# The second of three 768-token blocks makes its output products by Strassen's scheme, in an attention and feed-forward kernel

## The chip, the cores and the metric

The kernel runs on one core of one Trainium2 chip. The metric is device time in microseconds of one execution, the median of the runs shown. One execution was taken with the hardware profiler; where this text gives a start or a window, it is in microseconds from the first instruction of that execution.

## The reference

```
for c in range(24):                      # chunks of 32 queries, 8 heads of 64, 4 batches of 768
    k_full = concat(mem_k, k[c*32-16 : c*32+40]); v_full = concat(mem_v, v[same])
    s = (q_c @ k_full.T) / 8
    a = exp(s - max(s)); a = a / (sum(a) + 1e-9)
    out[c] = a @ v_full
x = out as 3072 tokens x 512             # 8 heads of 64 side by side
h = x @ w_in                             # 512 x 2048
g = max(h, 0) + alpha * min(h, 0)
result = g @ w_out                       # 2048 x 512
```

All arrays are float32. The two large products, x @ w_in and g @ w_out, are the bulk of the arithmetic. The kernel makes each of them from three reduced-precision products: every operand is split into a high part (rounded to fp32r) and a low part (the remainder, again fp32r), and low times high, high times low and high times high are added in PSUM. So each product step is three matmuls, and each operand costs one rounding copy (`high`, ScalarE) and one subtraction (`low`, VectorE or GpSimd).

## The kernel before

**Blocks.** The 3072 tokens are eight halves of 384 (BT). The first two halves are two plain blocks; the other six are three big blocks of 768 tokens, called big 0, big 1 and big 2 here (`big(s)`, L1209). Attention is made in 32 units (four pairs of heads for each half): the first eight ahead of everything, the rest between the matmuls, a few units at a time (`attend`, L535, and `meet`, L1580, which tables AT_PAIR and AT_REST place).

**Up.** A big block splits x into 2 by 2 quarters and w_in into slices; slice pair i holds the columns of two slices f = 2i and 2i+1. `pair` (L1404) makes the seven Strassen-Winograd products of one slice pair (B11, B21, T2, T3, T1, T4, B22), each six matmuls of 128x384 in `product`, L1418. It puts them together with one copy (L1431) and seven additions of a PSUM bank to an SBUF tile (`add_in`, L1439), and each of the four results is bent by alpha (`bent`, L1232 on ScalarE and L1235 on VectorE). The forms of x that the products multiply are differences of quarters (`forms`, L1070: `less` on GpSimd, L1073) and their high and low parts (`split_form`, L1048: L1055 and L1059). The forms of w_in are made by `sum_far` (L963) and kept in DRAM (far_a, far_b).

**Down.** Big 0 and big 1 make g @ w_out plainly: `chunk` (L1259) is three matmuls of 128x512 for one slice, half and 128-token tile, 96 chunks a block, with high and low parts from `rooms` (L1242). Big 2 makes it by Strassen's scheme: `form_down` (L1353) makes four differences of g for a slice pair on GpSimd (L1359), and `product_down` (L1363) makes a step of one product, three matmuls of 128x384 at L1372, for 7 products by 8 slice pairs by 2 column halves. Two of the seven products (A1, two steps each) run beside the pairs (`early_down`), five in `finish` (L1496), which adds the results (L1534) and writes the output transposed. The weights' forms S1 to S4 for this are made by `sum_far(..., down)` from loaded w_out slices (the additions at L982) while big 0 and big 1 run, and kept in DRAM (far_s).

**Order.** Nothing runs in the order of the code. Every step goes to `Plan.add` with an engine, a cost in microseconds, what it reads and writes and a due time; `Plan.send` (L198) then simulates five engines and one DMA queue and issues, on each engine, the ready step with the most work behind it. The table SHIFT moves single steps by microseconds. The result is one fixed instruction order for each engine. All large transfers go through SyncE's one queue, in order; an issue that waits for its data or its room holds the issues behind it.

**Rooms.** SBUF is shared out by hand. Weights of the pairs (1.79 MB a pair: `wa`) and of the down steps (`wo`, `ws`, 1 MB each) come from DRAM into seven slots (9 to 15), which the lists `queues` and LAST_ROOMS hand out; a slot is loaded again when its last matmul has read it. PSUM has eight banks: three for the products of a pair, three for down sums, two for attention scores.

## Time and profile before

| | us |
|---|---|
| median of 3 runs (574.44 to 578.03) | 576.23 |
| the profiled execution | 574.95 |
| its span, first to last instruction | 573.2 |
| TensorE busy in the span | 562.8 |
| VectorE, ScalarE, GpSimd busy | 428.2, 311.5, 195.3 |
| moved by DMA | 173.57 MB, mean 303 GB/s |

The span is 1.75 us shorter than the profiled execution's time, and that execution is 1.28 us under the median. Matmuls are pipelined: the mean duration of one overlaps the next, so the rate of a run of matmuls is its length over its count. Some matmul records are missing from the trace. "DMA share" is the mean busy share of the core's 16 DMA engines. Big 0 begins at about 165 (its pairs at 204), big 1 at 317, and the two blocks' work overlaps around 443 to 454, where big 2's pairs begin.

### The profile page before, as it was taken

Reading aid. Unit: us, or ns where it says so; the run is one execution under the profiler, and the core shown is the slowest. Engines: PE = TensorE matmul, PEld = TensorE weight load, DVE = VectorE, ACT = ScalarE, POOL = GpSimd, SP = SyncE. Lnnn points to the kernel's source line nnn. Section 1 sums busy time; section 2 is a strip of 40 time slices with the busy share of each in tenths; the row PEclk is TensorE's granted clock in tenths of the full one; section 3 lists DMA queues with packets and bytes.
Section 4 is the critical chain, followed back from the end, with each engine's and each line's share of the span. In section 5 each row is a group of like instructions: output and inputs, shape, how many; then the busy total and the mean of one; then the engine's idle time right before and its main releaser. Section 6 shows DMA issues by size and latency. Waiting matters only on the chain.

```text
span 573.2 us, 12065 instructions
## 1 busy us (share of the span) xinstructions
PE 562.8 (98%) x4515; PEld 509.2 (89%) x4515; DVE 428.2 (75%) x786; ACT 311.5 (54%) x792; POOL 195.3 (34%) x219
## 2 busy tenths in 40 slices
PE   7999999999999999999999999999999999999997
PEld 4789989888988899988888989999888899999997
DVE  7888888886648987666656777786855867787765
ACT  3778788775655663354566553543554543335452
POOL 5641000024375833005146511232533844443300
PEclk9999999999999999999999999999999999999999
DMA  8999954658996699987999999997988599778721
GB/s 310 374 417 419 414 238 184 227 216 293 335 377 251 231 393 409 377 322 259 326 365 331 351 382 327 355 313 287 312 290 280 198 339 353 279 241 332 266 84 56
DMA packets 64706, 173.57 MB, mean 303 GB/s; under 512 B 5768, under 2 KB 32520, under 8 KB 57736
## 3 DMA queue, kind: packets, MB, share of 16 engines
q1 hardware_dynamic: 64504, 172.70, 82.8%
q8 instruction: 36, 0.59, 0.4%
q14 instruction: 22, 0.18, 0.1%
q10 hardware_dynamic: 144, 0.10, 0.1%
HBM read 128.74 MB, written 44.04 MB: 301 GB/s over the span
## 4 chain that ended last, share of the span: by engine, by line
PE 88%; DMA 7%; DVE 2%; POOL 1%; issue 1%; ACT 0%; SPq 0%; DVEq 0%; POOLq 0%; ACTq 0%
PE b_ps L1418 25%; PE b_ps L1274 20%; PE o_ps L870 12%; PE h_ps L840 12%; PE b_ps L1372 10%; PE a_ps L528 3%; PE b_ps L1311 3%; DMA far_sS<-form 2%; PE s_ps L425 2%; DMA early<-heads 2%; DMA wa<-far_a 2%; DMA w_t<-w_out 1%; DVE u L1439 1%; PE a_ps L688 0%; POOL ew L663 0%
## 5 line engine op out<-in xcount | busy, mean ns | idle before, releaser
L1418 PE MATMUL b_ps<-xf,wa 128*128 128x384 f32 x924 | 168.1, 336 | 0.9 <-DMA wa<-far_a 0.9
L1418 PEld LDWEIGHTS b_ps<-xf,wa 128*128 128x128 f32 x924 | 161.1, 188 | 4.3 <-DVE gs L1235 1.3
L1439 DVE TENSOR_TENSOR u<-b_ps,u 128x384 f32<-128x384 f32 x154 | 79.5, 552 | 42.9 <-PE b_ps L1418 28.1
L1232 ACT ACTIVATE g<-u 128x384 f32<-128x384 f32 x88 | 45.5, 525 | 74.2 <-DVE u L1439 72.3
L480 POOL TENSOR_TENSOR e<-e,den 128x384 f32<-128x384 f32 x24 | 22.0, 919 | 137.5 <-DVE den L474 103.3
L840 PE MATMUL h_ps<-xh,w 128*128 128x384 f32 x256 | 65.4, 336 | 0.0
L1274 PE MATMUL b_ps<-wo,xh 128*128 128x512 f32 x180 | 55.9, 392 | 0.0
L1274 PE MATMUL b_ps<-wo,gh 128*128 128x512 f32 x180 | 55.9, 392 | 0.0
L870 PE MATMUL o_ps<-w,xh 128*128 128x512 f32 x168 | 52.5, 394 | 0.0
L840 PEld LDWEIGHTS h_ps<-xh,w 128*128 128x128 f32 x256 | 46.4, 188 | 0.8
L459 ACT ACTIVATE e<-s_ps,mx 128x64 f32<-128x64 f32 x144 | 43.1, 323 | 5.3 <-DVE mx L451 5.3
L840 PE MATMUL h_ps<-xl,w 128*128 128x384 f32 x128 | 43.7, 341 | 0.0
L1073 POOL TENSOR_TENSOR plain<-plain 128x384 f32<-128x384 f32 x24 | 29.4, 1238 | 36.6 <-ACT plain L602 29.7
L1274 PEld LDWEIGHTS b_ps<-wo,xh 128*128 128x128 f32 x180 | 33.8, 188 | 6.6
L1274 PEld LDWEIGHTS b_ps<-wo,gh 128*128 128x128 f32 x180 | 33.8, 188 | 6.5
L870 PEld LDWEIGHTS o_ps<-w,xh 128*128 128x128 f32 x168 | 31.5, 188 | 6.2
L1274 PE MATMUL b_ps<-wo,xl 128*128 128x512 f32 x90 | 35.4, 393 | 0.7 <-DVE xl L1252 0.7
L1274 PE MATMUL b_ps<-wo,gl 128*128 128x512 f32 x90 | 35.6, 395 | 0.0
L870 PE MATMUL o_ps<-w,xl 128*128 128x512 f32 x84 | 33.1, 394 | 0.0
L459 ACT ACTIVATION_READ_ACCUMULATOR e<-s_ps,mx 128x1 f32 x144 | 31.0, 215 | 0.0
L1059 POOL TENSOR_TENSOR xf<-plain,xf 128x384 fp32r<-128x384 f32 x24 | 27.0, 1142 | 11.3 <-ACT xf L1055 11.2
L852 DVE SCALAR_TENSOR_TENSOR g<-g,rise,h_ps 128x384 f32<-128x384 f32 x32 | 19.3, 607 | 12.5 <-ACT g L849 12.5
(166 smaller groups left out, 1129.6 us busy)
## 6 DMA issues: line engine op xcount, KB each, us to landing
wo<-far_o SPq DMA_DIRECT2D x24, 1024.0 KB
wa<-far_a SPq DMA_DIRECT2D x22, 1024.0 KB
wa<-far_b SPq DMA_DIRECT2D x22, 768.0 KB
qk<-qkw SPq DMA_DIRECT2D x24, 464.0 KB
w_t<-w_in SPq DMA_DIRECT2D x16, 512.0 KB
w_t<-w_out SPq DMA_DIRECT2D x16, 512.0 KB
far_o<-w SPq DMA_DIRECT2D x16, 512.0 KB
far_sS<-form SPq DMA_DIRECT2D x32, 256.0 KB
```

What stands on the lines that cost most here:

```text
L459: nc.scalar.activation(out=st["e"][:, i], in_=st["s"][h2][:, n], func=AF.Exp, scale=SCALE, bias=d["mx"][:, u - us[0], n, h2:h2 + 1], accum ...
L480: nc.gpsimd.tensor_tensor(out=st["e"], in0=st["e"], in1=st["den"].broadcast_to([P, NJ * 2, KW]), op=ALU.mult)
L840: nc.tensor.matmul(out=h["ps"][:, :BT], lhsT=ws[f, 0][:, wk, k * P:(k + 1) * P], rhs=parts(blk, k)[1](xk), start=(k == 0 and n == 0), stop ...
L852: nc.vector.scalar_tensor_tensor(out=h["g"], in0=h["g"], scalar=rise[:, f:f + 1], in1=h["ps"][:, :BT], op0=ALU.mult, op1=ALU.add)
L870: nc.tensor.matmul(out=o_ps[tt], lhsT=h[gk][:, tt * P:(tt + 1) * P], rhs=ws[f, 1][:, wk], start=(f == first_f and i == 0), stop=(f == last ...
L1059: eng.tensor_tensor(out=xf[x][:, 1, p], in0=plain_at(ap), in1=xf[x][:, 0, p].bitcast(F32), op=ALU.subtract)
L1073: step(POOL, 1.04, lambda: nc.gpsimd.tensor_tensor(out=plain_at(to[0]), in0=plain_at(a[0]), in1=plain_at(b[0]), op=ALU.subtract), reads=[a ...
L1232: nc.scalar.activation(out=h[name], in_=src(), func=AF.Relu, scale=-1.0)
L1274: nc.tensor.matmul(out=o[which][tt], lhsT=h[gk][:, tt * P:(tt + 1) * P], rhs=w[:, wk].bitcast(F32R), start=(f == turns[which][0] and i == ...
L1372: nc.tensor.matmul(out=o[0][bank[1]], lhsT=w[:, wk, m * P:(m + 1) * P].bitcast(F32R), rhs=forms_g[gk][xk], start=opened and k == 0, stop=c ...
L1418: nc.tensor.matmul(out=h[bank[1]][:, :BT], lhsT=weight(wk, p).bitcast(F32R), rhs=xf[xi][:, xk, p], start=p == 0 and k == 0, stop=p == 1 an ...
L1439: nc.vector.tensor_tensor(out=h[t], in0=h[bank[1]][:, :BT], in1=h[t if of is None else of], op=ALU.add)
```

## The change

Big 1 now takes the path of big 2: `finish` runs for both, with seven lower products over 8 slice pairs, and both write their output transposed. In both, only A11 (one product, `early_down`) runs beside the pairs; A12 is a sixth product of `finish` and is added onto A11's open PSUM banks, and S4 onto S1's (ONTO, LOWER). The fourteen weight loads of a block use five slots (ROOMS), since slots 14 and 15 now hold kept g tiles (`cell`). The form T3 of g is written to DRAM (far_t) and read back. In big 1 the forms T1 and T3 are made in the pair and T2 and T4 in `finish`; attention's last units are met between `finish`'s steps.

In `pair`, in all three blocks, the products come in another order: B21 is added onto B11's bank after B11 was copied out, and B22, put off until the next pair's first product was issued, onto T1's bank. Five additions remain of seven, and c11 is bent from PSUM.

The decoder writes decoded, unsplit weights to DRAM (far_raw, `keep_raw`): w_out's slices of the pairs 3 to 7, w_in's of 5 to 7. `sum_far` reads these (pairs 0 to 2 of w_out: the split parts, far_o) in place of weights in SBUF or of far_a and far_r, and most of the w_out sums move from big 1 into big 0. In `forms`, T3's low part and two of four differences move from GpSimd to VectorE. Outputs of big 0 leave through one buffer where three took turns. SHIFT is replaced as a whole (its entries are left out here).

```diff
-NROWS = B * S - 2 * BT
+NROWS = B * S - 4 * BT
...
-AT_PAIR = ({2: 16, 5: 18}, {1: 24, 4: 26}, {})
-AT_REST = ({2: 20, 9: 22}, {3: 28, 11: 30}, {})
+AT_PAIR = ({2: (16, 20), 5: (18, 22)}, {2: (None, 26), 6: (24, 28)}, {})
+AT_REST = ({2: (20, 24), 7: (22, None)}, {4: (26, 30), 16: (28, None), 28: (30, None)}, {})
...
-FIRST_LATE = 5
-LATE_AT = {(0, 0): 5, (0, 5): 6, (1, 3): 7}
-DOWN_AT = {(1, 2): 1, (1, 3): 2, (1, 4): 3, (1, 5): 4, (1, 6): 5}
-DOWN_REST = {(0, 4): 6, (0, 6): 7, (1, 2): 0}
+FIRST_LATE, FIRST_RAW = 5, 3
+LATE_AT, LATE_REST = {(0, 0): 5, (0, 4): 6}, {(0, 8): 7}
+DOWN_AT = {(0, 1): 3, (0, 2): 1, (0, 3): 2, (0, 5): 6, (1, 2): 5}
+DOWN_REST = {(0, 2): 4, (0, 5): 7, (0, 11): 0}
...
-LAST_ROOMS = ((13, "A1", 0), (14, "A1", 1), (15, "S1", 0), (13, "A1", 2), (14, "A1", 3), (13, "S1", 1), (9, "S2", 0),
-              (10, "S2", 1), (11, "S4", 0), (12, "S4", 1), (14, "S3", 0), (15, "S3", 1), (13, "A22", 0), (9, "A22", 1))
-LAST = (("S1", "T1"), ("S2", "T2"), ("S4", "c22"), ("S3", "T3"), ("A22", "T4"))
+ROOMS = ((13, "A11", 0), (13, "A11", 1), (9, "S1", 0), (10, "S1", 1), (11, "A12", 0), (12, "A12", 1), (13, "S4", 0),
+         (9, "S4", 1), (10, "S2", 0), (11, "S2", 1), (13, "S3", 0), (12, "S3", 1), (11, "A22", 0), (13, "A22", 1))
+LOWER = (("S1", "T1"), ("A12", "c21"), ("S4", "c22"), ("S2", "T2"), ("S3", "T3"), ("A22", "T4"))
+ONTO = ("A12", "S4")
+FROM = {"A11": (0, 0), "A12": (1, 0), "A22": (1, 1)}
...
-SHIFT = {("load_head", 1): 1.6, ("load_head", 7): 1.5, ("load", 0): 4.1, ("load", 4): -11.2, ("load", 15): 3,
...
+SHIFT = {("load_whole", 0): 12.8, ("load_head", 1): 3, ("load_values", 1): -1.5, ("move", 0): 2.3,
...
+    far_t = {(s, i): far.tile([P, BT], F32, name=f"far_t{s}{i}", tag=f"t{s}{i}") for s in range(1, NBIG) for i in range(NFP)}
+    far_raw = [far.tile([P, 2, DM], F32, name=f"far_raw{f}", tag=f"raw{f}") for f in range(NF)]
...
+        kept_raw = [i for i in parts if f >= 2 * (FIRST_RAW if i else FIRST_LATE)]
+
+        def keep_raw():
+            lo = parts.index(kept_raw[0])
+            move(out=far_raw[f][:, kept_raw[0]:], in_=d["a"].bitcast(F32)[:, lo:])
+
+        if kept_raw:
+            step(SP, 0.75, keep_raw, reads=[a], writes=[("raw", f, i) for i in kept_raw])
...
-    MORE = PLACES + [(sums, "r", [("rs", 0, 0), ("rs", 0, 1)])]
-    MORE += [(sums, f"s{i}", [("f", i, 0), ("f", i, 1)]) for i in range(2)]
-
-    def leave_at(late):
-        n = next(ntmp)
-        return MORE[n % (2, 3, len(MORE))[late]]
+
+    def leave_at(late=False):
+        return PLACES[0 if late else next(ntmp) % 2]
...
     far_b = [far.tile([P, 6 * HALF], F32, name=f"far_b{i}", tag=f"b{i}") for i in range(NFP)]
-    far_r = {i: far.tile([P, 4 * HALF], F32, name=f"far_r{i}", tag=f"r{i}") for i in range(FIRST_LATE, NFP)}
-    far_s = {(x, h): far.tile([P, NFP // 2, 2, HALF], F32, name=f"far_s{x}{h}", tag=f"s{x}{h}")
-             for x in ("S1", "S2", "S3", "S4") for h in range(2)}
-    far_o = [far.tile([P, 2, 2, DM], F32, name=f"far_o{i}", tag=f"o{i}") for i in range(NFP)]
+    far_s = {(x, h): far.tile([P, NFP // 2, 2, DM], F32, name=f"far_s{x[0]}{h}", tag=f"s{x[0]}{h}")
+             for x in (("S2", "S3"), ("S4", "S1")) for h in range(2)}
+    far_w = [far.tile([P, NFP // 2, 2, 2, DM], F32, name=f"far_o{h}", tag=f"o{h}") for h in range(2)]
+    far_o = [far_w[i // 4][:, i % 4] for i in range(NFP)]
 
...
-        if i >= FIRST_LATE:
-            send(f1, 0, ("dr", i), far_r[i])
...
-    def sum_far(i, gate, down=None):
-        late = down is None and i >= FIRST_LATE
+    def sum_far(i, gate, down=None, begin=0.0):
+        late = i >= (FIRST_LATE if down is None else FIRST_RAW)
+        both = down is not None and not late
+        which = int(down is not None)
...
+            if both:
+                formed(n)
+                move(out=t[n].bitcast(F32), in_=far_o[i][:, n])
+                return
+            begun(n)
+            move(out=r[n], in_=far_raw[2 * i + n][:, which])
...
-        def put_down(n, k2, x):
-            move(out=far_s[x, i // 4][:, i % 4], in_=t[n].bitcast(F32)[:, :, k2 * HALF:(k2 + 1) * HALF])
-
-        whole = [[("rs", n, 0), ("rs", n, 1)] + ([("f", n, 1)] if n or late else []) for n in range(2)]
-        if late:
...
+        for n in range(2):
+            if late:
+                step(SP, 0.75, partial(fetch, n), reads=gate + [("raw", 2 * i + n, which)], writes=whole[n], rest=begin)
+            else:
+                step(DVE, 0.7, partial(full, n), reads=gate + ([("f", n, 0), ("f", n, 1)] if both else [("w", 0, 2 * i + n, 0), ("w", 0, 2 * i + n, 1)]), writes=whole[n],
+                     port=True, rest=begin)
...
-        slow = ("B11", "B21", "T3", "T4")
+        slow = ("B11", "B21", "T4")
...
-            less(b12, b22, b12)
+            less(b12, b22, b12, True)
             split_form("T3", *b12, p)
-            less(b22, b22, b11)
+            less(b22, b22, b11, True)
             split_form("T2", *b22, p)
...
+        def go():
+            to = wa[x, b, h] = wps[f, 0].tile([P, n, 2, HALF], F32, name="ws", tag="w")
+            f01, k = FROM[x] if pair_of is None else (None, pair_of.index(x))
+            src = far_w[h][:, :, f01] if pair_of is None else far_s[pair_of, h]
+            move(out=to, in_=src[:, :, :, k * HALF:(k + 1) * HALF])
...
+    def cell(n, s):
+
+        if n < 6 or 14 <= n < 16:
+            f = NF // 2 + (n + 2 if n < 6 else n - 14)
+            to, key = keep_place(f)
+            return (lambda: plain_at(to)), [key]
+        f, b = divmod(n - 6, 2) if n < 14 else divmod(n - 16, 5)
...
+        def form_down(i, names):
+            for to, a, b in (("T1", "c12", "T1"), ("T3", "c22", "T3"), ("T2", "c22", "T1"), ("T4", "c21", "T2")):
+                if to not in names:
+                    continue
...
+                if to == "T3":
+                    step(SP, 0.75, lambda pt=pt: move(out=far_t[s, i], in_=pt()), reads=[kt], writes=[("dt", s, i)])
...
+        def fetch_form(i):
+            place, key = form_at("c22", i)
+            back["T3", i] = place, key
+            step(SP, 0.75, lambda: move(out=place(), in_=far_t[s, i]), reads=[("dt", s, i)], writes=[key])
...
-            for x in range(2):
-                room_of["A1", x, i] = room_of[2 * i + x]
-                forms_g["A1", x, i] = g[0, 2 * i + x]
-                for m in range(2):
-                    product_down("A1", i // 2, ("A1", x, i), i, low_banks[2 * x + m], m, i == 0, i == NFP - 1)
-            if i % 2:
-                load(home["A1", i // 2])
+            gk = "A11", i
+            room_of[gk] = room_of[2 * i]
+            forms_g[gk] = g[0, 2 * i]
+            for m in range(2):
+                product_down("A11", gk, i, lower[m], m, i == 0, i == NFP - 1)
+            if i % 4 == 3:
+                load(home["A11", s, i // 4])
...
-                                start=p == 0 and k == 0, stop=p == 1 and k == 2,
+                                start=not onto and p == 0 and k == 0, stop=p == 1 and k == 2, skip_group_check=onto,
...
             product(a, 0, w(0, 0), "B11")
             copy_out(0, a)
-            product(b, 0, w(0, HALF), "B21")
-            product(c, 0, w(0, 4 * HALF), "T2")
-            add_in(1, c, 0)
-            add_in(0, b)
-            first(h, "c11", 0, f0)
-            product(a, 1, w(1, 0), "T3")
-            add_in(2, a, 1)
+            end_pair()
+            product(b, 0, w(0, 4 * HALF), "T2")
+            add_in(1, b, 0)
+            product(a, 0, w(0, HALF), "B21", True)
+            first(h, "c11", lambda: h[a[1]][:, :BT], a[2], f0)
+            product(c, 1, w(1, 0), "T3")
+            add_in(2, c, 1)
             product(b, 1, w(1, HALF), "T1")
             add_in(0, b, 2)
-            add_in(1, b)
-            bent(h, "c22", lambda: h[0], ("tmp", 0), f1, *kept_at(f1))
-            product(c, 1, w(1, 4 * HALF, HALF), "T4")
-            add_in(2, c)
-            first(h, "c21", 2, f1)
-            product(a, 0, w(0, 5 * HALF), "B22")
-            add_in(1, a)
-            bent(h, "c12", lambda: h[1], ("tmp", 1), f0, *kept_at(f0))
-            if last:
-                form_down(i)
+            bent(h, "c22", lambda: h[0], ("tmp", 0), f1, *(claim("c22", i) if s else kept_at(f1)))
+            product(a, 1, w(1, 4 * HALF, HALF), "T4")
+            add_in(2, a)
+            first(h, "c21", lambda: h[2], ("tmp", 2), f1)
+            load(home["i", s, i, 1])
+
+            def rest_of_pair():
+                product(b, 0, w(0, 5 * HALF), "B22", True)
+                add_in(2, b, 1)
+                bent(h, "c12", lambda: h[2], ("tmp", 2), f0, *(claim("c12", i) if s else kept_at(f0)))
+                if s:
+                    form_down(i, ("T1", "T3", "T2", "T4") if last else ("T1", "T3"))
+                load(home["i", s, i, 0])
+
+            open_pair.append(rest_of_pair)
+            if s:
                 if i:
                     early_down(i - 1)
             elif i:
                 for f in (2 * i - 2, 2 * i - 1):
                     whole(0, f)
                 used(0, i - 1)
-            for x in range(2):
-                load(home["i", s, i, x])
...
-                at_, x = leave_at(1 if s == 0 else 0), {}
+                at_, x = leave_at(True), {}
...
+            for n, (x, name) in enumerate(LOWER):
+                banks = banks_of[x]
                 for i in range(NFP):
+                    at_ = n * NFP + i
+                    think()
+                    if at_ in AT_REST[s]:
+                        meet(AT_REST[s][at_], spare_banks)
                     if n == 0 and i == 2:
                         early_down(end)
                         for m in range(2):
+                            copy("a", m, lower[m])
                     take_down(x, name, i)
+                    if x == "S4":
+                        fetch_form(i)
+                    if x == "S1" and not last:
+                        form_down(i, ("T2",))
+                    if x == "A12" and not last:
+                        form_down(i, ("T4",))
+                    if last and x == "A22" and i >= NFP - NEND:
                         continue
                     for m in range(2):
+                        late_down(x, name, i, banks[m], m, i == 0 and x not in ONTO, i == end)
                     if i == 3 or i == end:
+                        load(home[x, s, i // 4])
                 for m in range(2):
+                    if x == "S1":
+                        copy("c", m, banks[m])
+                    elif x == "A12":
+                        copy("b", m, banks[m], (0, 0, m))
                     elif x == "S4":
+                        pass
+                    elif x == "S2":
+                        add("a", "a", m, banks[m])
+                        add("b", "a", m, upper[m], tile_no=(0, 1, m))
                     elif x == "S3":
+                        add("a", "a", m, banks[m])
+                        add("c", "c", m, other="a", tile_no=(1, 1, m))
+                    else:
+                        if last:
+                            for i in range(NFP - NEND, NFP):
+                                late_down(x, name, i, banks[m], m, False, i == end)
+                        add("a", "a", m, banks[m], tile_no=(1, 0, m), parts=1 + m if last else 1)
...
-        if last:
+        if s:
```

## Rows read from the trace of the kernel before

**Rows 1.** The page's busy time by engine: microseconds, share of span, instructions.
```profile
PE 562.8 (98%) x4515; PEld 509.2 (89%) x4515; DVE 428.2 (75%) x786; ACT 311.5 (54%) x792; POOL 195.3 (34%) x219
```

**Rows 2.** Busy time by stage: engines with instruction counts, granted clock, DMA share, GB/s.
```profile
core 0: us, PE busy (x) PEld busy (x) DVE busy (x) ACT busy (x) POOL busy (x), PEclk, DMA share, GB/s
...
165.00:317.00 152.00, 151.94 (x1370) 134.68 (x1356) 107.26 (x213) 82.77 (x272) 61.45 (x64) 1.00 0.91 329
317.00:386.00 69.00, 68.08 (x588) 63.24 (x588) 55.52 (x112) 34.36 (x103) 19.55 (x22) 1.00 0.99 348
386.00:454.30 68.30, 67.61 (x370) 58.27 (x370) 47.35 (x71) 30.04 (x60) 30.82 (x30) 1.00 0.79 280
454.30:523.70 69.40, 69.40 (x398) 68.87 (x397) 52.22 (x97) 27.87 (x56) 33.07 (x31) 1.00 0.83 300
523.70:573.20 49.50, 46.26 (x264) 45.38 (x263) 34.09 (x63) 22.64 (x46) 4.82 (x4) 1.00 0.45 159
```

**Rows 3.** Pieces of the chain that ended last: start, length, work.
```profile
273.38 10.26 PE b_ps L1274 x45
...
303.73 1.47 PE a_ps L528 x32
...
426.30 12.45 PE b_ps L1274 x54
...
469.61 7.28 PE b_ps L1418 x42
...
523.69 46.29 PE b_ps L1372 x264
```

**Rows 4.** Waits of the big blocks' matmuls (b_ps) on TensorE: total us, times, longest.
```profile
PE b_ps L1418 <- DMA wa<-far_a: 0.9, 1, 0.9
...
PE b_ps L1274 <- DVE xl L1252: 0.7, 1, 0.7
```

**Rows 5.** The DMA queue's packets, MB and share, 165 to 317 and 317 to 454.3.
```profile
q1 hardware_dynamic: 17180, 49.80, 90.3%
...
q1 hardware_dynamic: 16632, 42.94, 88.6%
```

**Rows 6.** What SyncE's queue waited for: total, times, longest.
```profile
SPq L322 <- DVE form L993: 26.4, 18, 4.0
```

**Rows 7.** Groups by line and shape: busy, mean ns; idle before and releaser.
```profile
L1439 DVE TENSOR_TENSOR u<-b_ps,u 128x384 f32<-128x384 f32 x154 | 79.5, 552 | 42.9 <-PE b_ps L1418 28.1 <-issue 8.3 <-ACT u L1431 3.2
...
L459 ACT ACTIVATE e<-s_ps,mx 128x64 f32<-128x64 f32 x144 | 43.1, 323 | 5.3 <-DVE mx L451 5.3
...
L459 ACT ACTIVATION_READ_ACCUMULATOR e<-s_ps,mx 128x1 f32 x144 | 31.0, 215 | 0.0
...
L1059 DVE TENSOR_TENSOR xf<-plain,xf 128x384 fp32r<-128x384 f32 x20 | 19.0, 972 | 7.6 <-ACT xf L1055 7.5
...
L1431 ACT COPY u<-b_ps 128x384 f32<-128x384 f32 x22 | 10.5, 480 | 22.2 <-PE b_ps L1418 20.2 <-DVE vg L1235 1.0 <-DVE qk L1235 1.0
...
L1534 DVE TENSOR_TENSOR o_t<-b_ps,o_t 128x384 f32<-128x384 f32 x13 | 7.1, 554 | 1.5 <-PE b_ps L1372 1.4
...
L1252 DVE TENSOR_TENSOR gl<-gs,gh 128x384 fp32r<-128x384 f32 x12 | 6.6, 555 | 4.4 <-ACT gh L1248 4.4
...
L982 DVE TENSOR_TENSOR sum<-wo 128x512 f32<-128x512 f32 x8 | 5.5, 684 | 1.1 <-DMA out<-o_t 1.1
...
L1248 ACT CAST gh<-gs 128x384 fp32r<-128x384 f32 x12 | 6.2, 516 | 9.2 <-PE b_ps L1274 7.1 <-PE b_ps L1372 2.1
...
L1359 POOL TENSOR_TENSOR gs<-gs 128x384 f32<-128x384 f32 x4 | 4.1, 1018 | 0.0
```

**Rows 8.** Timeline where VectorE and GpSimd both build forms: start, length, work.
```profile
443.46 2.65 DVE L1059 TENSOR_TENSOR xf<-plain,xf 128x384 fp32r<-128x384 f32 x2
...
441.79 3.90 POOL L1073 TENSOR_TENSOR plain<-plain 128x384 f32<-128x384 f32 x3 [0.56 <-DVE xf L1059]
```

380 lines of the change are left out of this document (206 added, 174 removed), and 37 rows, old and new, of the table SHIFT.

## The prediction

> **What bounds the kernel now.** I read the page's busy times first: TensorE is busy for 562.8 us of the 573.2 us span, no other engine above 75% [rows 1]. An average can hide a stage, so the table by stage comes next [rows 2]. From 165 to 523.7 TensorE is idle for 1.7 us in all, at granted clock 1.00 (the 2.4 GHz level); the last stage loses 3.2 us after its last matmul, the rest lies ahead of 165. The chain that ended last is, where big 0, 1 and 2 are concerned, nearly a list of matmuls back to back [rows 3], and the waits of their matmuls come to 0.9 and 0.7 us, one each [rows 4]. So time goes where TensorE's instruction time goes, as long as the others keep up. The second reading is how near they are: the DMA engines are 90.3% and 88.6% busy over big 0 and big 1 [rows 5], 99% from 317 to 386, and TensorE still lost only 0.9 us of those 69 [rows 2]. VectorE has a quarter of its time left.
>
> **Part 1, the output products of big 1.** Removed: 96 chunks of three matmuls of 512 columns. Their rate is 10.26/45 = 228 ns to 12.45/54 = 231 ns each [rows 3], so 288 take 65.7 to 66.4 us. Added: 7 products by 8 slice pairs by 2 column halves by 3 = 336 matmuls of 384 columns. The same instruction runs in big 2 at 46.29/264 = 175 ns, and the pairs' at 7.28/42 = 173 ns [rows 3]: 58.2 to 58.9 us. The difference is 6.8 to 8.2 us; I take **-7.5**. No other TensorE work changes: the pairs keep 42 matmuls each, attention's products are only met at other places.
>
> **Part 2, what Strassen asks of the others.** In `finish` of big 1 each step of TensorE (6 matmuls, 1.05 us) wants one rounding on ScalarE (516 ns) and one subtraction on VectorE (555 ns alone) [rows 7]. The half block is 48 such steps, one early step and three meetings of attention values at 1.47 us [rows 3]: 49 x 1.05 + 4.4 = 55.9 us. ScalarE: 48 + 14 (forms of big 2) roundings at 516 ns, 12 exponentials at 323 + 215 ns, 12 copies at 480 ns [rows 7] = 32.0 + 6.5 + 5.8 = 44.3 us, 79%. VectorE: 48 + 8 low parts and 4 differences at 555 ns, 10 additions at 554 ns = 33.3 + 5.5 = 38.8 us, some 70%, if nothing slows it. The 16 differences of g on GpSimd are 16.3 us at 1018 ns. From 454.3 to 523.7 VectorE was busy for 75% and GpSimd for 48% with no idle TensorE [rows 2], so I cost this at nothing; it is covered by the matmuls, and the second rival prices the case that it is not.
>
> **Part 3, pairs with five additions.** 22 pairs x 2 x 552 ns = 24.3 us leave VectorE [rows 7]. TensorE didn't wait for them (rows 4 have no such line), so this gives no time, only room. New waits: B21 goes onto B11's bank, so it waits for ScalarE's copy of 480 ns [rows 7]; between them lie B22 of the pair before and T2, 2 x 1.04 us of cover (6 matmuls at 173 ns). c11 is read from PSUM by two engines, and T4 wants that bank two products later: an estimated 1.2 us of reading (a copy's 480 ns and an addition's 552 to 684 ns [rows 7] as the nearest rows) under 2.1 us. Both hold unless ScalarE's queue is over a microsecond late; bounds 0 and 0.5 us a pair, I take 0, because the old order gave the same copy two products before T3 took its bank, and shows no wait. T2 is now wanted as the second of a pair's own products, so a block's first pair wants the forms earlier. Its chain (difference 1018, rounding 516, low part 972 ns [rows 7]) is 2.5 us; units 22 and 23 are met two slices sooner (two slices are 18 matmuls, 4.1 us), and steps of the block before can stand in. 0 to 2.5 us, I take 0.
>
> **Part 4, the weight sums.** The raw additions drop from 32 to 16, 16 x 684 ns = 10.9 us off VectorE [rows 7], again not on the path. The price is in DMA. Over big 0 and big 1: the three late w_in sums fetch 2 x 0.26 MB in place of 2 x 0.52 (-1.6 MB); the eight w_out sums, which read slots before, fetch 3 x 1.05 + 5 x 0.52 MB (+5.8); big 1 loads 14 weight tiles for 13 (+1.0); T3 goes out and comes back, 16 x 0.197 MB (+3.1). Together +8.4 MB. The queue moved 92.7 MB there in 0.903 x 152 + 0.886 x 137.3 = 258.9 busy us [rows 5], 2.79 us a MB: 23.4 us more, 282.3 busy us in a stretch of 289.3 - 7.5 = 281.8 us. So the change takes all the room that the DMA engines had. From 317 to 386 they were 99% busy and cost TensorE one wait of 0.9 us [rows 2, 4]; bounds are 0 and the 23.4 us. I take one more such wait, **+0.9**, being nearest to that stage.
>
> The sums move from big 1 to big 0, in SyncE's order past the pairs' loads. A put waits for its low part, 18 times for 1.5 us and at most 4.0 [rows 6], and the loads of `wa` stand behind it. There are now 16 puts of 512 KB for 32 of 256 KB, and 16 fetches more. A `wa` slot has a pair and two slices (7.3 + 4.1 us) to be filled in big 0 and 8.3 us in big 1; 1.88 MB take 5.2 us. A 4 us hold is about what is left, so it is covered, barely. The decoder's ten puts of raw weights (4.2 MB, for 1.6 of far_r) fall before 165. Single buffer for big 0's outputs: three copies and transfers in a row of 0.26 MB (0.7 us each and the way there); the first early step on those banks comes two pairs later, 14 us: nothing.
>
> **Sum.** -7.5 + 0.9 = -6.6: span 566.6 us, execution 568.4 with the 1.75 us around it. The profiled execution stands 1.28 us under the median of 576.23, so the median comes to **569.6 us**.
>
> **Rival 1, the DMA queue becomes the bound (slower).** Place: 165 to 446. Before, 30.4 of 289.3 us were gaps, in which nothing was ready or an issue waited. The demand is 282.3 busy us, so every microsecond of gap that remains is a microsecond longer. If half remain, the stretch is 297.5 us, 8.2 longer than before: 584.4 us. It passes 582 from 12.8 us of gaps on. For it: the fetch, form, put chain of a sum lies in one set of buffers and must idle; 165 to 317 is where demand rises most. Against: 317 to 386 ran without gaps, the sums have until big 1's `finish`, 66 us into it, and much of the rise can be put off to 386 to 454, where the share was 79% [rows 2]. Chance 0.15.
>
> **Rival 2, GpSimd and VectorE hold each other up in big 1's lower half (no change).** Where both build forms, three GpSimd differences took 3.90 us and two VectorE low parts in the same time 2.65 [rows 8], 1.3 us a pair for operations that take 1.02 and 0.555 alone [rows 7]. The half has 28 GpSimd operations (16 differences of g, 6 low parts, 4 differences of x, 2 scalings) and 60 VectorE operations of that kind: 28 x 1.3 + 32 x 0.555 = 54.2 us, and 59.7 with the additions from PSUM behind them, against TensorE's 55.9. So the wait is 0 to 3.8 us, and up to 2.5 more where big 2's first pair finds T2 late: with 5 us, 573.7. For it: the two differences and T3's low part that move to VectorE. Against: in 454.3 to 523.7 GpSimd made 31 operations beside 97 of VectorE without a wait [rows 2]. Chance 0.18. The Trainium skill (SBUF — State Buffer, "SBUF: two separate sides") says that a VectorE operation with two SBUF inputs and a GpSimd operation that reads SBUF take one port pair in turn, each for its whole length, which speaks against moving work between these two; by that rule alone the half would be 28 x 1.02 + 60 x 0.555 = 61.9 us, 6.0 over, and the kernel at 574.7. The pair of 1.3 us agrees with it to within 0.3.
>
> **Rival 3, it gains more.** The two waits of 1.6 us lie in replaced code [rows 4]; with them gone, no new one and 8.2 us of part 1, the span is 563.4, the median 566.4. Chance 0.07. That the change doesn't do what it says is excluded by part 1's rates, unless 336 matmuls are not what runs.
>
> **How the numbers follow.** The forecast's case has 0.60. One per cent is 5.8 us, about what a measurement of this kernel can tell from no change; the bound is 570.5, only 0.9 over my number, so of that 0.60 I put 0.45 to faster and 0.15 to within. Rival 1 gives 0.10 slower, 0.05 within; rival 2 0.16 within, 0.02 faster; rival 3 0.07 faster. Faster 0.54, same 0.36, slower 0.10. Range: rival 3 less a microsecond for its scatter, 565.5, up to rival 2 at its full price and rival 1 with up to 9 us of gaps, 578. The forecast's own range is 566.5 to 573.
>
> **What would show it.** In the changed profile: 228 ns matmuls of 512 columns gone from big 1 and some 672 at L1372's successor at 175 ns in both blocks; 110 additions in the pairs for 154; TensorE idle 165 to 523 under 3 us; DMA share near 1.0 in big 0 and 1. Wrong if TensorE waits for `wa`, `ws` or forms for over 3 us there (rival 1: for DMA; rival 2: for VectorE's or GpSimd's forms about 425 to 455), or if it gains time ahead of 165, which I count as unchanged.

## The result, and the profile after

| | before | after |
|---|---|---|
| median of 9 runs each, us | 575.50 (573.53 to 578.93) | 580.22 (579.30 to 581.53) |
| span of the profiled execution, us | 573.2 | 579.2 |
| mean granted clock of TensorE in it | 1.000 | 0.997 |
| moved by the SyncE queue, MB | 172.70 | 186.86 |

The ratio is 1.0078, 95% interval 1.0053 to 1.0103: the kernel became 0.8% slower, where 1.1% faster was forecast. 580.22 lies outside the range. Here and below, each ratio compares a kernel with runs of the kernel before on the same chip, so ratios, and not medians, are set against each other. One run each of e1, e4 and e8 and the profiled one of e5 (774.6 us at a clock of 0.657) were disturbed and are in no ratio.

The page's line of busy times, which answers to [rows 1]:

```profile
PE 558.5 (96%) x4563; PEld 514.4 (89%) x4563; DVE 437.5 (76%) x774; ACT 323.1 (56%) x820; POOL 213.6 (37%) x233
```

TensorE has 48 matmuls more and is busy 4.3 us less; its idle time went from 10.4 to 20.7 us. So -4.3 + 10.3 make the 6.0 us of the span. The table by stage shows where, with the columns of [rows 2]; big 1 now ends at 459.4 where it ended at about 454 (twelve of its matmuls came later, among big 2's pairs):

```profile
core 0: us, PE busy (x) PEld busy (x) DVE busy (x) ACT busy (x) POOL busy (x), PEclk, DMA share, GB/s
165.00:317.00 152.00, 149.62 (x1338) 132.20 (x1337) 110.69 (x206) 80.47 (x251) 59.10 (x63) 1.00 0.97 352
317.00:386.00 69.00, 61.78 (x530) 57.67 (x529) 48.40 (x97) 35.48 (x122) 31.01 (x34) 0.98 0.99 347
386.00:460.00 74.00, 72.96 (x487) 71.38 (x486) 60.54 (x94) 42.38 (x89) 40.65 (x34) 1.00 0.97 334
460.00:529.00 69.00, 68.40 (x395) 68.11 (x394) 52.62 (x87) 27.30 (x55) 30.47 (x29) 1.00 0.79 271
529.00:579.20 50.20, 46.96 (x271) 46.64 (x269) 30.38 (x54) 23.37 (x47) 4.87 (x4) 1.00 0.74 243
```

Two stages hold most of it: 2.4 us of TensorE are idle in big 0 and 7.2 between 317 and 386, where it was 0.1 and 0.9; that is 8.6 of the 10.3 us. The two last stages are as long as they were, within 0.7 us. The DMA share is 0.97 to 0.99 in all three stages of big 0 and big 1, where it was 0.91, 0.99 and 0.79. The queue's packets, MB and share from 165 to 317 and from 317 to 460, as in [rows 5]:

```profile
q1 hardware_dynamic: 17602, 53.31, 96.9%
...
q1 hardware_dynamic: 27800, 48.43, 97.7%
```

That is 101.74 MB in 147.3 + 139.7 = 287.0 busy us of 295. Before it was 92.74 MB and 258.9 of 289.3. The gaps fell from 30.4 to 8.0 us, and the stretch still grew: 5.1 us to its end at 459.4, most of the loss.

TensorE's longest waits in the big blocks, the successors of [rows 4] (total us, times, longest):

```profile
PE b_ps L1528 <- DVE u L1549: 2.8, 3, 1.4
PE a_ps L592 <- DMA pt<-far_e: 2.6, 2, 2.1
PE b_ps L1477 <- ACT o_t L1598: 2.4, 1, 2.4
PE b_ps L1477 <- DVE gl L1343: 1.7, 1, 1.7
PE b_ps L1528 <- DMA wa<-far_a: 0.6, 1, 0.6
```

Only two of the five name a transfer. The timeline shows what the others wait for (start, length, engine, line, idle time before it and its releaser); here for `o_t` and `gl`:

```profile
330.61 0.59 ACT L1598 COPY o_t<-b_ps 128x512 f32<-128x512 f32 x1
331.22 0.34 SPq L386 DMA_DIRECT2D out<-o_t  x1
...
338.59 0.58 ACT L1598 COPY o_t<-b_ps 128x512 f32<-128x512 f32 x1 [3.67 <-DMA out<-o_t]
...
339.23 0.44 PE L1477 MATMUL b_ps<-xl,ws 128*128 128x384 f32 x1 [2.39 <-ACT o_t L1598]
...
343.32 3.18 POOL L1067 TENSOR_TENSOR sum<-sum 128x256 f32<-128x256 f32 x4 [1.46 <-DMA sum<-far_raw]
...
345.78 0.49 ACT L1323 ACTIVATE g<-b_ps 128x384 f32<-128x384 f32 x1 [2.87 <-PE b_ps L1528]
...
347.40 0.69 DVE L1075 TENSOR_TENSOR form<-sum,form 128x512 fp32r<-128x512 f32 x1
...
348.08 0.63 ACT L1072 CAST form<-sum 128x512 fp32r<-128x512 f32 x1
...
348.70 1.02 POOL L1457 TENSOR_TENSOR plain<-gw,plain 128x384 f32<-128x384 f32 x1 [2.20 <-DVE gw L1326]
...
348.75 1.52 DVE L1075 TENSOR_TENSOR form<-sum,form 128x512 fp32r<-128x512 f32 x1
...
350.66 0.88 DVE L1343 TENSOR_TENSOR gl<-gs,gh 128x384 fp32r<-128x384 f32 x1
...
351.59 0.44 PE L1477 MATMUL b_ps<-gl,ws 128*128 128x384 f32 x1 [1.69 <-DVE gl L1343]
```

Big 0's third output waits 3.67 us on ScalarE, since the one buffer is still being written out: issued at 331.22, the write let the next copy start at 338.59. The early product wants that PSUM bank, and TensorE stands for 2.39 us. For `gl` no transfer comes last. A late weight sum gets its raw tile late, but its merges are done at 346.50, and ScalarE, which waited 2.87 us for the products behind the first wait, rounds the second of its two tiles only at 348.08. On VectorE g's low part stands behind the sum's low part. That one takes 1.52 us where the first tile's took 0.69, and g's takes 0.88 where it takes 0.55 alone; GpSimd works beside both. These 1.2 us are most of the wait of 1.69.

Two of the three waits for `u` come from another fetch:

```profile
354.93 4.18 SPq L386 DMA_DIRECT2D form<-far_o  x2
363.47 0.69 DVE L1064 TENSOR_TENSOR sum<-form 128x512 f32<-128x512 f32 x1 [2.18 <-DMA form<-far_o]
365.88 0.69 DVE L1064 TENSOR_TENSOR sum<-form 128x512 f32<-128x512 f32 x1 [1.19 <-DMA form<-far_o]
367.10 3.52 PE L1528 MATMUL b_ps<-xf,wa 128*128 128x384 f32 x18 [1.37 <-DVE u L1549]
```

VectorE waits 2.18 and 1.19 us for fetched weights, with the pair's additions queued behind. A low part of the same sum holds up the next one, 0.74 us at 371.35. So three of the five (`pt`, `o_t`, `wa`) and most of `u` start at a transfer that comes late, and `gl` follows from them and from VectorE and GpSimd side by side.

### The profile page after: what moved, and what is told of

Read it like the earlier page. It is cut to its first block, busy times and chain, and to the rows that moved or that the text cites. A ratio compares the mean times of both kernels' runs of the same rounds, so it can differ in the third digit from the quotient of the medians.

```text
span 579.2 us, 12352 instructions
## 1 busy us (share of the span) xinstructions
PE 558.5 (96%) x4563; PEld 514.4 (89%) x4563; DVE 437.5 (76%) x774; ACT 323.1 (56%) x820; POOL 213.6 (37%) x233
## 3 DMA queue, kind: packets, MB, share of 16 engines
q1 hardware_dynamic: 86008, 186.86, 89.8%
## 4 chain that ended last, share of the span: by engine, by line
PE 69%; DMA 22%; DVE 3%; ACT 2%; issue 2%; SPq 1%; POOL 1%; DVEq 0%; ACTq 0%; POOLq 0%
PE b_ps L1528 19%; PE b_ps L1477 18%; PE h_ps L914 12%; PE o_ps L944 11%; PE b_ps L1365 5%; DMA pt<-far_e 4%; DMA far_a<-form 3%; DMA far_e<-et 3%; DMA out<-o_t 2%; PE a_ps L592 2%; PE s_ps L489 2%; SPq L386 1%; DMA w_t<-w_out 1%; DMA wo<-far_o 1%; DMA wa<-far_a 1%
## 5 line engine op out<-in xcount | busy, mean ns | idle before, releaser
L1549 DVE TENSOR_TENSOR u<-b_ps,u 128x384 f32<-128x384 f32 x110 | 60.7, 552 | 20.8 <-PE b_ps L1528 19.0
L1067 POOL TENSOR_TENSOR sum<-sum 128x256 f32<-128x256 f32 x49 | 40.9, 835 | 48.4 <-DVE sum L1064 34.2
L1477 PE MATMUL b_ps<-xh,ws 128*128 128x384 f32 x224 | 57.1, 336 | 0.0
L1477 PE MATMUL b_ps<-gh,ws 128*128 128x384 f32 x224 | 56.9, 334 | 0.0
L1477 PEld LDWEIGHTS b_ps<-xh,ws 128*128 128x128 f32 x224 | 40.8, 189 | 0.0
L1477 PE MATMUL b_ps<-xl,ws 128*128 128x384 f32 x112 | 38.0, 339 | 2.7 <-ACT o_t L1598 2.4
L1477 PEld LDWEIGHTS b_ps<-gh,ws 128*128 128x128 f32 x224 | 40.4, 188 | 0.0
L1477 PE MATMUL b_ps<-gl,ws 128*128 128x384 f32 x112 | 37.9, 338 | 1.7 <-DVE gl L1343 1.7
L1323 ACT ACTIVATE g<-b_ps 128x384 f32<-128x384 f32 x30 | 14.8, 492 | 37.3 <-PE b_ps L1528 30.7
L1343 DVE TENSOR_TENSOR xl<-plain,xh 128x384 fp32r<-128x384 f32 x36 | 28.2, 791 | 6.3 <-ACT xh L1339 5.7
```

Source lines behind the costliest of these rows:

```text
L1067: nc.gpsimd.tensor_tensor(out=part(*to), in0=part(*a), in1=part(*b), op=op)
L1323: nc.scalar.activation(out=h[name], in_=src(), func=AF.Relu, scale=-1.0)
L1343: (nc.gpsimd if slow else nc.vector).tensor_tensor(out=h["gl"], in0=src(), in1=h["gh"].bitcast(F32), op=ALU.subtract)
L1477: nc.tensor.matmul(out=o[0][bank[1]], lhsT=wa[x, s, h][:, i % 4, wk, m * P:(m + 1) * P].bitcast(F32R), rhs=forms_g[gk][xk], start=opened a ...
L1549: nc.vector.tensor_tensor(out=h[t], in0=h[bank[1]][:, :BT], in1=h[t if of is None else of], op=ALU.add)
```

## The experiments

Theory A: the added bytes fill the queue, and that is the loss. Rivals: the single output buffer (C); the changed kernel's order on VectorE and ScalarE around the late sums (D), or of the products themselves (E); the changed kernel's table of shifts (F); and, found on the way, that the queue of the kernel before already keeps back part of what faster products give (G). Microseconds worked out from a ratio are (ratio - 1) x 575.

### What bytes cost with nothing else changed

**More bytes in the kernel before (e7).** Transfers of 0.59 MB from DRAM to DRAM behind the pairs' loads, 14 of them.

```diff
+            if into and x[3] == 1 and x[1] < NBIG - 1:
...
+                to = far.tile([P, 1152], F32, ...)
+                move(out=to, in_=far_a[x[2]][:, :1152])
...
```

> The kernel before in its own order, and with each far_b load of big 0 and big 1 (14) one more transfer of 0.59 MB from DRAM to DRAM that nothing waits for: 8.3 MB, as much as the change adds there. Theory A: DMA share goes to 96 to 100% from 165 to 454 and the kernel gets 4 to 10 us slower than before, 579 to 585 us. Theory B (the bytes don't matter, the new order does): under 1.5 us slower.

583.70 us, ratio 1.0141 (1.0092 to 1.0189): +8.1 us for 8.3 MB that nothing waits for. In its trace the queue is 95.5% busy from 165 to 317 and 92.9% from 317 to 454 (90.3% and 88.7% before), a little under what was expected. Two of the names among TensorE's waits, `wa` and `u`, are those of the changed kernel:

```profile
PE b_ps L1423 <- DMA wa<-far_a: 2.4, 1, 2.4
PE b_ps L1279 <- DVE u L1444: 1.6, 1, 1.6
PE b_ps L1423 <- DVE u L1444: 1.1, 2, 0.6
PE b_ps L1279 <- DVE xl L1257: 1.1, 1, 1.1
```

Of the 9.0 us that its span is longer, 5.7 are idle time of TensorE and 3.3 are busy time of the same 4515 matmuls (566.1 us for 562.8). Behind the wait of 2.4 us the granted clock fell to 0.50. Of its four runs, the one at a mean clock of 1.000 has a span of 576.9 us, the three at 0.993 to 0.997 have 581.7 to 583.2. So the price of 8.1 us holds part of what the low clock costs.

**The products' gain alone (e14), with more bytes (e15), and both with fewer (e16, e17).**

```diff
   # e14, e15, e17: big 1 (s is 1), second and third matmul of a chunk
-                        out=o[which][tt],
+                        out=o[which][tt] if not s or not i else o[which][tt][:, :424],
...
-                        rhs=w[:, wk].bitcast(F32R),
+                        rhs=w[:, wk].bitcast(F32R) if not s or not i else w[:, wk, :424].bitcast(F32R),
   # e16, e17: 32 puts of weight sums, and their loads
-  move(out=far_s[...], in_=t[n]...[:, :, k2 * HALF:(k2 + 1) * HALF])
+  nc.sync.dma_start(out=far_s[...][:, :, :32], in_=t[n]...[:, :, k2 * HALF:k2 * HALF + 32])
-  move(out=to, in_=far_s[x, h])
+  move(out=to..., in_=far_o[h]...)   # same size
```

> The kernel before, with the products' gain alone: of the 288 output matmuls of big 1 the second and third of each chunk, 192 in all, take 424 of the 512 columns, which is 192 x 229 ns x 88/512 = 7.6 us less of TensorE (these columns miss two of their three terms); no transfer and no other instruction changes. Theory A with the products' gain whole: a span of 565.5-567, ratio 0.986-0.989. Theory G (the queue of the kernel before already paces big 1, so that faster products only wait for it): 568.5-571, with new waits for wa.

> The fourteenth and the seventh experiment together: the products' gain and 8.3 MB of transfers that nothing waits for, in the kernel before. If gain and price are two terms of a sum, 583.7 less 7.6: 576. If the shorter stretch makes the queue tighter still, 578-582, as the changed kernel's 580.

> The kernel before with 7.3 MB less: its 32 puts of weight sums write 32 of 256 columns each, and the eight loads of those sums read decoded weights of the same size instead (so that the values are other ones); all instructions and their order stay. Theory A with the queue's room as price on both sides: the kernel before has only 1.7 us of idle TensorE where these bytes lie, so the time falls by 0 to 2 us, ratio 0.996-1.000. A fall of over 4 us would say that more than waits is paid for bytes.

> The same with the narrow products of the fourteenth experiment (7.6 us less of TensorE). Theory G (the queue kept back what was missing there): now the whole 7.6 us is there beside the sixteenth, a ratio 0.013 lower than its own, 0.983-0.987. If it isn't the bytes: the ratio of the fourteenth again, 0.990-0.994.

| queue, MB against before | products as before | narrow products |
|---|---|---|
| -7.3 | 0.9980 (0.9960 to 1.0000), e16 | 0.9861 (0.9823 to 0.9900), e17 |
| 0 | 1 | 0.9918 (0.9888 to 0.9948), e14 |
| +8.3 | 1.0141 (1.0092 to 1.0189), e7 | 1.0069 (1.0035 to 1.0103), e15 |

Taking 7.3 MB away gives 1.2 us, adding 8.3 costs 8.1. As the prices of a byte these have a knee at the load of the kernel before. That it is the load and not the place isn't shown: the bytes taken away are puts of weight sums, the added ones stand behind the pairs' loads. The narrow products' own rate, in the chain of e14 (start, length, work, number), is 3.10 / 15 = 207 ns where it was 229, so they are 288 x 22 ns = 6.3 us shorter, not 7.6:

```profile
347.88 3.10 PE b_ps L1274 x15
```

Of these 6.3 us the span shows 3.1 in e14 (570.1 for 573.2) and 6.4 in e17 (564.6 for e16's 571.0). The ratios say 4.7 and 6.8, with overlapping intervals, so I go by the waits in the traces. First e14's waits, then e17's:

```profile
PE b_ps L1418 <- DMA wa<-far_a: 1.6, 2, 0.9
PE b_ps L1274 <- DVE xl L1252: 1.5, 1, 1.5
```

```profile
PE b_ps L1419 <- DMA wa<-far_b: 0.4, 1, 0.4
PE b_ps L1275 <- DMA wo<-far_o: 0.3, 1, 0.3
```

Theory G fits the traces: with the bytes of before the faster products ran into 2.0 us more of such waits (0.5 of it for `u`); with fewer they didn't. The times alone don't show it. And e15, the gain and the bytes in the kernel before's own order, lands at +4.0 us, the change at +4.5. **Shorter products and more bytes alone are enough for a result of this size.** Its longest wait is for the pairs' weights:

```profile
PE b_ps L1423 <- DMA wa<-far_a: 3.7, 1, 3.7
```

The last row of the table also says what the shorter products still give with the added bytes: e15 is 4.1 us below e7 (1.0069, 1.0035 to 1.0103, against 1.0141, 1.0092 to 1.0189), about as much as e14's 4.7. Gain and price add up, -4.7 + 8.1 = 3.4 for 4.0; that a fuller queue keeps back more of the gain isn't seen.

### Taking the bytes and the buffer out of the changed kernel

**Fewer bytes (e1, e2).** The sums fetch 64 of 512 columns of their first raw tile and of the split parts (-4.6 MB), in e2 T3 also makes its round trip with 48 of 384 (-10.1 MB in all).

```diff
-            move(out=r[n], in_=far_raw[2 * i + n][:, which])
+            move_some(r[n], far_raw[2 * i + n][:, which], 64)   # n == 0
-            move(out=place(), in_=far_t[s, i])
+            move_some(place(), far_t[s, i], 48)                 # e2, and its put
```

> The changed kernel in the same instruction order, but the weight sums fetch only 64 of 512 columns of what they read from DRAM into the first raw tile and into the split parts (4.6 MB less moved; the sums are therefore wrong). Theory A (the DMA queue became the bound, its lateness reaches TensorE): 4.6 MB at 2.8 us a MB are 13 busy us, TensorE's idle time from 165 to 529 falls from 11 us to 5 to 8 us, time 575 to 578 us. Theory B (the new fixed order and the engines' own queues are late, not the bytes): within 1 us of the changed kernel's 580.2.

> As the run before, and the form T3 goes to DRAM and comes back with 48 of 384 columns (10.1 MB less than the changed kernel in all, so fewer bytes than the kernel before; wrong in the rest of T3). Theory A: idle from 165 to 529 under 4 us, 569 to 573 us. Theory B: 579 to 580.5 us.

578.21 (1.0041, 1.0011 to 1.0071) and 576.03 us (1.0037, 1.0007 to 1.0066). By the ratios about half of the loss goes, at the edge of the noise; bytes alone don't undo it. (e2 moves 176.77 MB, 4.1 more than the kernel before and not fewer, as its expectation has it.) The output buffer's wait stays, 3.1 us in both.

**The output buffer (e3, e4, e5, e6).** In e3 big 0's last three outputs go through ScalarE's queue, e4 is that with e2; in e5 they write 128 of 512 columns from separate quarters of the buffer, so that no copy waits for a transfer, and e6 is e5 with e2.

```diff
-                move(out=rows(r), in_=x["t"])
+                (nc.scalar if which else nc.sync).dma_start(out=rows(r), in_=x["t"])   # e3, e4
-                x["t"] = at_[0].tile([P, DM], F32, ...)
+                x["t"] = apart_o["t"][:, tt * P:(tt + 1) * P]                          # e5, e6
```

> The changed kernel in the same order, but the three last output tiles of big 0 (one buffer in a row) leave through ScalarE's DMA queue instead of SyncE's. If the single buffer behind SyncE's long queue causes TensorE's wait of 2.4 us at 339 and the half clock for some 3 us after it, both go: 576 to 577.5 us. If that wait only hides others behind it (theory A in full): 579 to 580.5 us.

> The smaller transfers of the second run and the output path of the third together. Theory A with the output buffer as a second place: idle from 165 to 529 under 3 us, 568 to 571 us, the time that the matmul counts give. Theory B: 576 to 578 us.

> The changed kernel in the same order; the last three output tiles of big 0 are copied and sent with 128 of their 512 columns, each into its own quarter of the one buffer, so that no copy waits for a transfer (three quarters of these outputs stay unwritten). Theory C (the single output buffer holds ScalarE, and through it TensorE, at about 339): that wait of 2.4 us and the half clock after it go, 2.5 to 5 us less than the changed kernel's 580.2. Theory A (bytes): the wait goes, others take its place, 579 to 580.5 us.

> The last run's output quarters together with the small sum fetches and the small T3 of the second run. If bytes and the output buffer are all that was missing: 568 to 571 us, idle from 165 to 529 under 4 us. If the order itself holds waits (low parts of sums ahead of low parts of g on VectorE at 351, 1.7 us, and the like): 571 to 574 us.

e3: 583.45 us, 1.0152 (1.0112 to 1.0192), slower still. The other queue doesn't make the transfer shorter; the third copy waits as long:

```profile
331.55 0.34 ACTq L1603 DMA_DIRECT2D out<-o_t  x1
339.62 0.59 ACT L1598 COPY o_t<-b_ps 128x512 f32<-128x512 f32 x1 [3.86 <-DMA out<-o_t]
```

e4: 579.09 us, 1.0077 (1.0051 to 1.0104), no better than the change. e5: 581.54 us, 1.0113 (1.0084 to 1.0142); with the buffer's wait made impossible nothing is gained, so C alone is refuted (no trace of e5 is used). e6: 575.25 us, 1.0005 (0.9985 to 1.0025): bytes and buffer together are worth 4.2 us of the change's 4.5, the buffer's 0.3% of them (e6 against e2) being within the noise. The longest wait left in e6's trace:

```profile
PE b_ps L1493 <- DVE gl L1359: 3.8, 1, 3.8
```

**The order around the late sums (e8, e9, e12, e13).** e8 is e6, e9 the changed kernel, with the late sums' merges and low parts made small; e12 is the changed kernel, e13 is e6, with g's rounding and low part sent ahead of the sum's.

```diff
-            nc.vector.tensor_tensor(out=t[n][:, 1], ...)          # e8, e9
+            nc.vector.tensor_tensor(out=t[n][:, 1, :64], ...)     # late sums; merges 32 of 256
+AHEAD = (("high", 124), 0), ((("high", 154), 0), (("low", 154), 0))     # e12, e13
...
+            if self.names[n] == AHEAD[0][0]:
+                for name, fn2 in AHEAD[1]:
...
+                    self.steps[m][2]()
```

> The sixth experiment's kernel, and in it the engine work of the late weight sums made small as well: GpSimd's merges over 32 of 256 columns, VectorE's low parts over 64 of 512 (the values of the sums are wrong; the instructions, their order and their number stay). In the sixth experiment's kernel the one long wait of TensorE that was left, 3.8 us at 343 us for VectorE's low part of g, stood behind two of these low parts, which wait for ScalarE's copies and these for GpSimd's four merges of 3.5 us. Theory D (what is left of the loss is that chain, in the order in which VectorE has it): the wait falls below 1 us, the span from 573.5 to 569.5-571.5, ratio to before 0.991-0.997. Theory E (the order of the matrix products themselves leaves holes there, whatever the sums cost): 573-574 again, with the wait at the same place for another thing.

> The changed kernel with nothing but that engine work of the late sums made small; all transfers stay at their full size. Theory A (the queue's bytes hold the stretch from 165 to 446 us): a span of 577-579.5, ratio to before 1.003-1.008, since a sum that is ready earlier finds the same queue. Theory D alone (the engine work and its order, not the bytes): 573-576.

> The changed kernel with two instructions sent earlier: ScalarE's rounding of that part of g which the product at 351.59 us waits for, and VectorE's low part of it, stand ahead of the late weight sum's rounding and low part instead of behind them; all else is as it was. Theory D (that order costs the wait of 1.7 us): the wait goes, 576.5-578 us of span. Theory A (the bytes pace the stretch): the time comes back at the next wait for a transfer, 578.5-579.5.

> The same in the sixth experiment's kernel (first raw tiles, split parts and T3 fetched in small, outputs apart, one output of big 0 written by a quarter of its columns), where that wait was 3.8 us. If bytes, output buffer and this order are all that took the products' gain: 573.5 less 3.8, and 1 to 2 less because the clock doesn't dip behind the wait: a span of 568-570, ratio to before 0.988-0.992. If there is more: 571.5-573.5.

e8: 574.23 us, 1.0000 (0.9972 to 1.0028). The wait is still there with 3.2 us, since the raw tile that the merges need comes late:

```profile
341.22 1.25 POOL L1084 TENSOR_TENSOR sum<-sum 128x32 f32<-128x32 f32 x4 [3.56 <-DMA sum<-far_raw]
346.80 0.56 PE L1495 MATMUL b_ps<-gl,ws 128*128 128x384 f32 x1 [3.22 <-DVE gl L1361]
```

e9: 580.77 us, 1.0105 (1.0051 to 1.0159): without the bytes gone, lighter sums give nothing, so the sums' engine work alone is not the cause. e12: 582.82 us, 1.0117 (1.0080 to 1.0154). The time isn't better than the change's. Two of its ten runs had spans of 573.9 and 575.8 at a clock of 1.000 and 0.999, the other eight 578.3 to 582.4 at 0.991 to 0.997. The trace is of the first; the wait for `gl` is gone there, and no trace shows the eight. e13: 573.46 us, 1.0003 (0.9964 to 1.0043). Here too `gl` is gone, and another took its place, so the expected 568 to 570 didn't come:

```profile
PE b_ps L1557 <- DMA wa<-far_a: 6.3, 3, 2.8
```

**Far fewer bytes (e18).** e6, with the 16 puts of the forms S1 to S4 at 64 of 512 columns and their loads taken from decoded weights, as in e16.

> The sixth experiment's kernel with 7.3 MB less again, as in the sixteenth: the 16 puts of the forms S1 to S4 write 64 of 512 columns, and the loads of these forms read decoded weights of the same size. Theory A (bytes alone account for what is left of the loss): as e17, a ratio of 0.984-0.990. Theory D (the changed kernel's order holds waits that come whatever the queue carries, the one of 3.8 us for g's low part first): 0.993-1.000, with that wait still there.

572.65 us, 0.9959 (0.9938 to 0.9980), with 168.84 MB, 3.9 below before. Its profiled execution had a span of 568.4 at clock 1.000. Its busy TensorE and the wait that is left:

```profile
PE 554.6 (98%) x4563; PEld 512.6 (90%) x4563; DVE 440.6 (78%) x774; ACT 322.0 (57%) x820; POOL 214.9 (38%) x233
...
PE b_ps L1494 <- DVE gl L1360: 2.2, 1, 2.2
```

TensorE's instructions are 8.2 us shorter than before, so the products' gain is there. It comes out as 2.4 us by the ratio, which lies in D's band, with the wait still there. Within this wait the sum's low part again takes 1.37 us for 0.69, with GpSimd at work. e17 gave 8.0 us, but the queue is not as free here: from 317 to 454 it is 87.6% busy, against 80.8% in e17 and 88.7% in the kernel before, though both move about 39 MB. First e18, then e17:

```profile
q1 hardware_dynamic: 29455, 39.78, 87.6%
```

```profile
q1 hardware_dynamic: 17542, 38.83, 80.8%
```

So the fair neighbour is e14, at 90.4% and 89.7% with shorter products in the old order, which gave 4.7 us. The 2.3 us between them would be the new order's, with intervals that overlap.

### The tables of shifts (e10, e11)

```diff
-SHIFT = {("load_whole", 0): 12.8, ...}
+SHIFT = {}
```

> The kernel before with its table of hand-found shifts of due times emptied, so that the planner's own order stands. It serves as the base of the next run. Expected slower than before by 10 to 40 us, since the table was fitted to this kernel.

> The changed kernel with its own table emptied. Theory F (the table of the changed kernel fits it worse than the other table fits the kernel before, and the change itself would pay): at least 3 us faster than the kernel before without a table. Theory A (the added transfers cost more than the products give back, however the work is ordered): 3 to 8 us slower than the kernel before without a table.

595.88 us (1.0395, 1.0331 to 1.0459) and 598.36 us (1.0425, 1.0384 to 1.0467). Each table is worth about the same, 22.7 us and 24.4 - 4.5 = 19.9. F isn't borne out: the change doesn't pay without them either. The intervals overlap, so the 3 to 8 us slower of A aren't shown.

## Why the prediction was wrong

**Part 1 was right.** In the chain after, 150 of the new matmuls take 26.20 us, 175 ns each, as the forecast had from big 2:

```profile
427.17 26.20 PE b_ps L1477 x150
```

336 x 175 ns against 288 x 229 ns is -7.2 us for -7.5, and e18 at clock 1.000 shows -8.2 in all. That TensorE's busy time fell by 4.3 only is partly the clock: the drop described below makes about 1.7 us of it.

**Part 2 was right, and rival 2 didn't come where it was placed.** In big 1's lower half VectorE is busy for 82 and 81%, and GpSimd for 87% up to 427. There VectorE's low parts take up to 1.37 us beside GpSimd's 1.33, like the pairs of 1.3 us that rival 2 counted with. But the 1.0 us that TensorE is idle are waits for `ws`, for `pt` and for its own products, none for a form:

```profile
400.00:427.00 27.00, 25.96 (x217) 24.85 (x216) 22.26 (x25) 16.93 (x36) 23.37 (x20) 1.00 1.03 342
427.00:460.00 33.00, 33.00 (x194) 32.91 (x191) 26.79 (x49) 18.17 (x38) 6.51 (x6) 1.00 0.95 337
```

What rival 2 described cost time earlier, where the forecast didn't look: in the wait for `gl` at 351.59.

**Part 4's price of the bytes failed: "I take one more such wait, +0.9, being nearest to that stage".** Measured, 8.3 MB cost 8.1 us in the old order (e7), and taking bytes and buffer out of the changed kernel gives back 4.2 (e6 against the change). e7's price is 1.0 us a MB, where e16 gives 0.16 below the load of before. The forecast's own sum already said it: 282.3 busy us in a stretch of 281.8 leaves no room for a gap, and there were 30.4 us of gaps. The stage with 99% share and one wait [rows 2, 4] was the wrong neighbour. It stood between stages at 0.91 and 0.79, where the loads could be early or late; in the kernel after no such stage is left before 460. e16 shows the other side: the same row was right that the kernel before paid little, 1.2 us, for what it carried. A price read at one load was used at another. (A pair's weights are 1.84 MB by the list of transfers, where the forecast wrote 1.88; nothing hangs on it.)

**Rival 1 is what happened to the queue**, at less than its half: up to 460 demand and gaps are 287.0 + 8.0 = 295 us, for 282.3 + 15.2 forecast. That sum holds for any stretch; what makes the queue a cause are e6, e7 and e15. The gaps shrank further than half, and the demand was larger, with 9.0 MB more instead of 8.4 and 2.82 us a MB for 2.79. Part 1's gain isn't lost in the queue as a whole: in e14, and in e15 against e7, the shorter products still gave 4.7 and 4.1 of their 6.3 us.

**Part 4's "nothing" for the output buffer, and Part 3's 0 for new waits, failed too.** Set against e14, the new order is a second loss of the size of the bytes': with the bytes of before in the stretch (93.4 MB to 454, for 92.7) and no wait for the buffer, the changed kernel is level with the kernel before, 1.0005 (0.9985 to 1.0025), where e14 has 0.9918 (0.9888 to 0.9948). (The queue is 94.3% and 90.5% busy in e6, 90.4% and 89.7% in e14, so a part of it may still be the queue's.) So from e14's -4.7 us the order leads to +0.3 and the bytes and the buffer to the +4.5 measured. The buffer was costed at 0.7 us a transfer "and the way there"; the first two took 6.1 and 7.3 us, together more than the 13.2 us from the first copy at 323.60 until TensorE came, which the forecast had about right with 14. It shows as a wait of 2.39 us, but it is worth nothing while the queue is full (e5), and when it is not, its 0.3% (e6 against e2) is within the noise. Part 4 asked what a late put holds up on SyncE. It didn't ask what a late fetch holds up on VectorE, where the sum's first addition stands ahead of the pair's: that is most of the 2.8 us for `u`. SyncE's hold itself was as forecast, 21.8 us for the 26.4 of [rows 6]:

```profile
SPq L386 <- DVE form L1075: 21.8, 21, 4.4
```

The 110 additions in the pairs for 154 came as said, with the same 552 ns [rows 7]; no time came with them, as forecast.

```profile
L1549 DVE TENSOR_TENSOR u<-b_ps,u 128x384 f32<-128x384 f32 x110 | 60.7, 552 | 20.8 <-PE b_ps L1528 19.0
```

**Still open.** e15 shows that shorter products and bytes suffice for a loss of this size. The opposite isn't shown: without the bytes the changed kernel is level (e6) or keeps 2.4 us (e18). What in the new order costs the rest, some 5 us in e6 and 2 in e18, isn't found. e6's wait of 3.8 us for `gl`, behind which the clock fell to 0.50 for some 3 us, is of that size, and so are e18's waits of 2.2 us for `gl` and 1.1 us for `pt`. But taking `gl` away from e6 (e13) brought up `wa`. E, the order of the products themselves, wasn't separated from D: e8 kept its time and its wait at the same place, as E said, but behind a transfer. Nor were VectorE and GpSimd kept apart, or single transfers moved in the order.

## What to carry to other kernels

When a change trades engine time for transfers, set the queue's busy time after the change, plus the gaps that a loaded queue still has (8 of 295 us here), against the stretch as the change would leave it; what is over is the size of the price to expect. Here 282.3 + 8 against 281.8 gives 8.5 us, for 8.1 in e7 and 4.2 in the changed kernel. Engine time saved there is seen only in part, and a new order has a price of its own, of the same size here. A stage at 99% with one short wait doesn't show that bytes are free when its neighbours have room. For each new transfer ask on which engine its first reader stands, and what is queued behind it there.
